# The first set of the second attention cut by units of 512 tokens, two of them spread by TensorE

## The chip, the cores and the metric

One core of a Trainium2 chip runs the whole program. The metric is device microseconds (us) for one execution; a kernel's figure is the median over its runs.

## The reference

Attention over a set of 32 learned points, and a gated feed-forward layer on its result:

```python
B, N, C, m = 4, 12416, 128, 32               # x (B, N, C), inducing I (m, C)
def mab(q, kv):                              # softmax attention, scale 1/sqrt(C)
    s = scale * (q @ kv.T); s = s - s.max(-1); a = exp(s); a /= a.sum(-1) + 1e-09
    return a @ kv
h = mab(I, x)                                # first attention:  32 points look at 12416 tokens
y = mab(x, h).reshape(B * N, C)              # second attention: each token looks at the 32 rows of h
xn = y / sqrt(mean(y * y, -1) + 1e-06) * rms_g
g, val = xn @ w_gate, xn @ w_val             # 128 -> 1536
out = (g * sigmoid(g) * val) @ w_out         # 1536 -> 128, float32, 49664 tokens
```

The weights arrive as 64-bit floats and are rounded to 32 bits in the kernel, by chunks of 512 columns.

## The kernel before

**Tiles.** A batch has 97 row tiles of 128 tokens, in 7 sets (five of 16 tiles, one of 15, one of 2). For the second attention and the feed-forward layer the sets are cut into units of 512 tokens or fewer: 25 in a batch, 100 in all. A unit's hidden columns come in 12 blocks of 128, so there are 1200 blocks.

**Second attention, folded.** `y` is never formed. With `a` the 32 attention weights of a token, the gate is `a @ (h * rms_g @ w_gate)`, so the kernel builds stacks `sg` and `sv` (`stack_of` L485, `stack_copy` L488, `stack_low` L492) that hold `h*g @ w_gate` and `h*g @ w_val`, an upper part and its remainder, and multiplies them with a unit's tile `a` of 128 partitions: upper, lower, upper and lower half of its 32 weights. The weights need no sum: the mean square of `y` goes through a 32x32 `gram` matrix (`square`, `times`, `total`, `clamp`), its power -0.5 is taken on GpSimd (`root`, L1032), and the weights are multiplied by it (`apply`, L1037).

**A block.** Gate matmul (L709), silu on ScalarE (L719), value matmul (L737), product on VectorE (L751), then the projection with `w_out`: either one plain f32 matmul (L807, kind P, two records) or, in the kinds S and D, three fp32r matmuls (L795, L796, L807) on parts that ScalarE (L764), VectorE (L770) and GpSimd (L815) prepare.

**Order.** Each engine takes its instructions in program order, and that order is written out by hand. The string `ORDER` in `first()` (from L890) lists every step up to the first block for batch 0: `t`/`a`/`v` transposes of x on TensorE and their copies on ScalarE/VectorE, `s` scores, `m` eviction with maximum, `e` exponentials, `r` transposes of them, `h` sums over tokens (`sum_h` L953), letters `p P u U g l j q` steps of the weights' rounding, then `fold`, `by` (`weigh` L966), `turn_h` (L972), `hT` (L977), and the second attention of set 0. That set is done here in two halves of 256 columns: `sc` (scores, L994), `T` (transpose, L998), `rm` (maximum, L1001), `sub` (L1006), `ex` (L1010), `ta`, `sq`, `zm`, `sm`, `mm` (L1029), `rt`, `ap`, `tb`, `hi`, `lo`. `sd` and `cp` spread unit 0 with a selection matrix on TensorE; `gather1` and `gather2` bring units 1 and 2 by DMA (`gather` L647: four transfers of 64 KB from the halves `hi` and `lo` on SyncE's queue, two each). Set 0's unit q consists there of the 32-partition groups q of all its columns.

What follows the first gate is given by long strings: `banks` (which bank of PSUM a step takes), `workers` and `outputs` (which buffer), `sorts` (the kind of each projection), `program` (one letter for each instruction of the blocks), and `taken` (which of the numbered small steps from `later()` and `seams()`, such as the weights' later chunks, other sets' second attention and the next batch's first attention, comes at each `.`). Each time a unit's tile is due, the iterator `gathered` gives the next unit to gather.

Of the kernel before, what the change touches and what calls it, by code (L numbers as in the profile page):

```python
# [23 lines left out]
def kernel(  # L24
# [101 lines left out]
    mhalf = small.tile([P, 16], F32, name="rt", bufs=1)  # L126
# [16 lines left out]
    sel = up.tile([P, 512], F32R, name="u", tag="u7")[:, 0:2 * P].rearrange("p (k r c) -> p k r c", k=2, r=R)  # L143
    nc.gpsimd.memset(sel.bitcast(F32), 0.0)
    for k in range(R):
        nc.gpsimd.tensor_copy(out=sel[:, k % 2, k, :], in_=ident[:, 0:m])
# [27 lines left out]
    def fetch_raw(i, c):  # L174
        if wide:
            raw[i, c] = words = places.pop(0).bitcast(I32)
            places.append(words.bitcast(F32))
            nc.sync.dma_start(out=words if i < 2 else words.rearrange("p (j c) -> p j c", j=512 // C),
                              in_=source(i, c).bitcast(I32))
# [8 lines left out]
    def rounding(i, c):  # L188
# [4 lines left out]
        def put():  # L193

            if i < 2:
                nc.sync.dma_start(out=w32[i][c][:], in_=st["dst"])
            if unread:
                fetch_raw(*unread.pop(0))
# [68 lines left out]
    NB, turn, turns, works, outs, factors = 5, [0], [], [int(c) for c in "01201212"], [int(c) for c in "01010"], []  # L267

    def bank():
        if turns:  # L270
            n = turns.pop(0)
        else:
            n = turn[0] % NB
            turn[0] += 1
        return pall[:, n, :]
# [8 lines left out]
    def attention(b, load_next):  # L284
# [129 lines left out]
        def scale_h():  # L414
            hg = st["hg"] = once.tile([P, P], F32, name="hg")
            nc.vector.tensor_scalar_mul(out=hg[:], in0=st["hT"][:], scalar1=gam)

        def square_h():

            if not b:  # L420
                scale_h()
# [217 lines left out]
    def gather(b, u):  # L639
# [4 lines left out]
        a = moving[b, u] = (xnp.tile([P, 512], F32R, name="xn1") if (b, u) == (0, 2) else  # L644
                            astk.tile([P, 512], F32R, name="a"))
# [210 lines left out]
    def store():  # L856
# [4 lines left out]
        if s == full:  # L861
            d = out[ds(b * N + start[s], P * per[s]), :].rearrange("(i w) c -> i w c", i=m)
        else:
            d = of(out, b, s)[q]
# [14 lines left out]
    GROUPS = ((0, 1, 2), (3, 4), (5, 6))  # L879
    ORDER = """  # L880
        open w3 t02 t00 t03 v00 t01 a01 a03 v02 t10 a10 t12 t13 s0 a12 a13 t11 t20 t21 a20 t23 m0 a23 t22 a22 a21 v11
        s1 t32 m1 t30 s2 a32 t33 t31 p00 P00 v30 u00 m2 own0 g00 Uv00 mB0 t40 l00 j00 q00 t42 nb0 a31 a33 t41 a40 v42 e0 t43
        s3 t51 a41 v43 s4 m3 e2 t52 t53 r0 t50 a51 m4 t60 own1 mB1 e1 a53 a50 a52 h0 r2 nb1 e3 p10 P10 r1 u10 U10 a60
        s5 h1 r3 m5 p20 e4 g10 s6 m6 h2 ls0 own2 mB2 u20 p11 nb2 ls1 r4 e5 least share r5 h3 h4 e6 ls2 shared fold h5
        r6 h6 l10 j10 q10 by0 by1 by2 P20 g20 u11 turn_h hT sc0z sc1z U20 l20 j20 q20 T0z rm0z sub0z ex0z T1z gram ta0z w7 sq0z rm1z
        sub1z ex1z zm0z ta1z sm0z st1 sq1z mm0z zm1z P11 silu sm1z mm1z rt0z rt1z p01 st0 U11 ap0z low0 tb0z
        ap1z hi0z tb1z lo0z w12 sd0z hi1z P01 cp0z lo1z w1 sd1z u01 cp1z w3 gather1 gather2
    """

    def first():  # L890

        V, S, G, T = nc.vector, nc.scalar, nc.gpsimd, nc.tensor
        st, at = f["st"], {}
# [5 lines left out]
        sums = pall[:, 7, :]  # L899
# [12 lines left out]
        def copy(copier, s, k):  # L912
            dst, src = at.pop(("turned", s, k))
            copier(out=dst, in_=src)
# [8 lines left out]
        def own_max(g):  # L923
            sets = GROUPS[g]
            t = at["own", g] = small.tile([P, R, R], F32, name="own")[:, :, 0:len(sets)]
# [3 lines left out]
        def spread_max(g):  # L929
            n = len(GROUPS[g])  # L930
            ps = bank()
            at["max"] = ps[:, 0:R * n]
# [3 lines left out]
        def bias_of(g):  # L936
            V.tensor_reduce(out=nb[:, g:g + 1], in_=at["max"], axis=AX.X, op=ALU.min)
# [9 lines left out]
        def sum_h(s):  # L947
# [3 lines left out]
            for t in range(per[s]):  # L951
                begin, end = (one[t % R] == (s, t) for one in ends)
                T.matmul(sums[ts(t % R, m), ts(group[s], C)], e[:, ts(t, m)], xn[:, t, :], start=begin, stop=end)  # L953
# [11 lines left out]
        def weigh(g):  # L965
            V.tensor_scalar(out=hs[:, ts(g, C)], in0=sums[:, ts(g, C)], scalar1=share[:, g:g + 1], scalar2=st["rl"][:],  # L966
                            op0=ALU.mult, op1=ALU.mult)

        def turn_h():
            ps = at["h"] = bank()  # L970
            for g in range(len(GROUPS)):
                T.matmul(ps[:, 0:P], hs[:, ts(g, C)], fold[:].rearrange("p q m -> p (q m)"), start=not g,  # L972
                         stop=g == len(GROUPS) - 1)

        def copy_h():
            hT = st["hT"] = once.tile([P, P], F32, name="hT")
            V.tensor_copy(out=hT[:], in_=at["h"][:, 0:P])  # L977

        H, HT = 2, per2[0] // 2
        a0 = {}  # L980

        def both(k):
            return slice(k * HT * m, (k + 1) * HT * m), slice(k * HT, (k + 1) * HT)

        def whole(name, make):
            if name not in a0:
                a0[name] = make()
            return a0[name]

        def scores2(k):  # L990
            cols, _ = both(k)
            ps = at["scores2", k] = bank()[:, 0:HT * m]
            for q in range(R):
                T.matmul(ps[ts(q, m), :], st["hT"][:, 0:m], xT[0, 0][:, q * per2[0] * m + cols.start:q * per2[0] * m + cols.stop],  # L994
                         start=True, stop=True)
# [4 lines left out]
        def row_max(k):  # L1000
            V.reduce_max(out=whole("mx", lambda: small.tile([P, 32], F32, name="mx2"))[:, both(k)[1]], in_=weights(0, 0)[:, both(k)[1], :],  # L1001
                         axis=AX.X)

        def sub_max(k):
            v = weights(0, 0)[:, both(k)[1], :]
            V.tensor_tensor(out=v, in0=v, in1=a0["mx"][:, both(k)[1]].unsqueeze(2).to_broadcast((P, HT, m)), op=ALU.subtract)  # L1006
# [5 lines left out]
        def turn_a(k):  # L1012
            V.transpose(out=whole("eT", lambda: worker([P, 512], F32, "eT"))[:, both(k)[0]], in_=sc[0][:, both(k)[0]])

        def square(k):
            ps = at["square", k] = bank()[:, 0:HT * m]
            T.matmul(ps, gram[0][:], a0["eT"][:, both(k)[0]], start=True, stop=True)

        def times(k):
            V.tensor_tensor(out=whole("z", lambda: worker([P, 512], F32, "z"))[:, both(k)[0]], in0=at.pop(("square", k)),  # L1020
                            in1=a0["eT"][:, both(k)[0]], op=ALU.mult)

        def total(k):
            V.reduce_sum(out=whole("ms", lambda: small.tile([P, 16], F32, name="ms"))[:, both(k)[1]],
                         in_=a0["z"][:, both(k)[0]].rearrange("p (t m) -> p t m", m=m), axis=AX.X, apply_transpose=True)

        def clamp(k):
            ms = a0["ms"][:, both(k)[1]]
# [466 lines left out]
```

## Time and profile before

| | |
|---|---|
| median of 3 runs | 1477.3 us (1476.86 to 1478.0) |
| the profiled execution's own time | 1478.17 us |
| its span in the trace | 1476.3 us |
| granted TensorE clock | 0.999 |
| TensorE matmul (PE) busy | 1464.3 us, 99%, 7290 instructions |
| VectorE (DVE) busy | 1428.1 us, 97%, 2484 |
| GpSimd (POOL) busy | 1366.7 us, 93%, 1197 |
| ScalarE (ACT) busy | 1302.0 us, 88%, 2596 |
| HBM | 53.95 MB read, 27.00 MB written |

PEld is TensorE's weight load, which runs beside its matmuls; SP is SyncE, and SPq, DVEq and so on are engines' DMA or instruction queues. "L709" is line 709 of the kernel. A row of the timeline has: start in us from the span's beginning, length, engine, line, operation, output<-input tile, shapes, a count where equal instructions follow each other, and in brackets how long the engine stood idle ahead of it and what ended that. A row with a count stretches from the first of the group to the last one's end, other instructions between them included. Busy time counts pipelined matmuls with modelled ends, so that 99% is not 99% of TensorE's peak.

### The profile page before, as it was taken

Reading aid. Unit: us, or ns where it says so; the run is one execution under the profiler, and the core shown is the slowest. Engines: PE = TensorE matmul, PEld = TensorE weight load, DVE = VectorE, ACT = ScalarE, POOL = GpSimd, SP = SyncE. Lnnn points to the kernel's source line nnn. Section 1 sums busy time; section 2 is a strip of 40 time slices with the busy share of each in tenths; the row PEclk is TensorE's granted clock in tenths of the full one; section 3 lists DMA queues with packets and bytes.
Section 4 is the critical chain, followed back from the end, with each engine's and each line's share of the span. In section 5 each row is a group of like instructions: output and inputs, shape, how many; then the busy total and the mean of one; then the engine's idle time right before and its main releaser. Section 6 shows DMA issues by size and latency. Waiting matters only on the chain.

```text
span 1476.3 us, 26012 instructions
## 1 busy us (share of the span) xinstructions
PE 1464.3 (99%) x7290; PEld 1102.3 (75%) x7290; DVE 1428.1 (97%) x2484; ACT 1302.0 (88%) x2596; POOL 1366.7 (93%) x1197
## 2 busy tenths in 40 slices
PE   9999999999999999999999999999999999999998
PEld 6566777877777777786777777777777777777787
DVE  6999999999999999999999999899999999999998
ACT  5798889889988889988988898988898999999997
POOL 1489998999999999999999999989989999999998
PEclk9999999999999999999999999999999999999999
DMA  7675324458544232455764212263332122122222
GB/s 286 130 118 104 64 43 94 88 124 130 84 85 79 36 65 37 99 132 106 125 106 99 44 37 36 44 135 91 74 63 46 33 37 43 37 39 41 42 39 34
DMA packets 391712, 116.28 MB, mean 79 GB/s; under 512 B 365584, under 2 KB 370704, under 8 KB 389008
## 3 DMA queue, kind: packets, MB, share of 16 engines
q1 hardware_dynamic: 390976, 114.55, 39.7%
q8 instruction: 58, 0.95, 0.3%
q14 instruction: 86, 0.70, 0.2%
q10 hardware_dynamic: 592, 0.08, 0.0%
HBM read 53.95 MB, written 27.00 MB: 55 GB/s over the span
## 4 chain that ended last, share of the span: by engine, by line
PE 95%; DVE 2%; ACT 1%; DMA 0%; issue 0%; POOL 0%; SPq 0%; DVEq 0%; POOLq 0%; ACTq 0%
PE gv L807 31%; PE gv L709 17%; PE gv L737 17%; PE gv L795 12%; PE gv L796 12%; PE gv L316 3%; PE gv L369 1%; PE gv L908 1%; DVE u L751 1%; PE gv L569 1%; PE gv L463 0%; PE gv L152 0%; DMA a<-lo 0%; POOL xn L815 0%; SPq L647 0%
## 5 line engine op out<-in xcount | busy, mean ns | idle before, releaser
L719 ACT ACTIVATE silu<-gv 128x512 f32<-128x512 f32 (+2 forms) x1200 | 673.8, 593 | 86.3 <-PE gv L709 69.6
L815 POOL TENSOR_TENSOR xn<-xn,xn 128x512 fp32r<-128x512 f32 (+2 forms) x467 | 579.1, 1256 | 22.4 <-PE gv L796 17.2
L709 PE MATMUL gv<-a,sg 128*128 128x512 f32 (+2 forms) x1188 | 482.1, 433 | 1.9 <-DMA a<-lo 1.5
L737 PE MATMUL gv<-a,sv 128*128 128x512 f32 (+2 forms) x1188 | 448.9, 410 | 0.2 <-ACT silu L719 0.2
L751 DVE TENSOR_TENSOR gv<-silu,gv 128x512 f32<-128x512 f32 (+2 forms) x658 | 431.4, 674 | 4.7 <-ACT silu L719 1.9
L764 ACT ACTIVATE xn<-gv 128x512 fp32r<-128x512 f32 (+2 forms) x633 | 371.0, 597 | 36.2 <-DVE gv L751 27.7
L751 DVE TENSOR_TENSOR u<-silu,gv 128x512 f32<-128x512 f32 (+2 forms) x542 | 345.4, 655 | 8.2 <-ACT silu L719 3.9
L807 PE MATMUL gv<-u,wo 128*128 128x512 f32 (+2 forms) x716 | 353.0, 577 | 0.1
L770 DVE SCALAR_TENSOR_TENSOR xn<-xn,gv 128x512 fp32r<-128x512 f32 (+2 forms) x520 | 339.6, 664 | 5.5 <-ACT xn L764 3.4
L709 PEld LDWEIGHTS gv<-a,sg 128*128 128x128 f32 x1188 | 223.6, 189 | 109.2 <-issue 36.6
L737 PEld LDWEIGHTS gv<-a,sv 128*128 128x128 f32 x1188 | 223.2, 189 | 85.8 <-issue 23.4
L815 POOL TENSOR_TENSOR xn<-xn 128x512 fp32r<-128x512 f32 (+2 forms) x216 | 268.8, 1252 | 9.1 <-PE gv L796 7.7
L777 POOL TENSOR_TENSOR xn<-u,xn 128x512 fp32r<-128x512 f32 (+2 forms) x163 | 202.1, 1245 | 13.6 <-ACT xn L761 9.2
L815 POOL TENSOR_TENSOR u<-xn,u 128x512 fp32r<-128x512 f32 (+2 forms) x130 | 163.2, 1260 | 2.6 <-PE gv L796 2.3
L795 PE MATMUL gv<-xn,xn 128*128 128x512 f32 (+2 forms) x430 | 163.5, 380 | 0.0
L807 PEld LDWEIGHTS gv<-u,wo 128*128 128x128 f32 x716 | 133.3, 190 | 28.3 <-issue 10.4
L807 PE MATMUL gv<-xn,xn 128*128 128x512 f32 (+2 forms) x366 | 141.1, 393 | 0.0
L796 PE MATMUL gv<-xn,xn 128*128 128x512 f32 (+2 forms) x366 | 136.5, 373 | 0.0
L795 PE MATMUL gv<-xn,more 128*128 128x512 f32 (+2 forms) x356 | 135.8, 381 | 0.0
L761 ACT ACTIVATE xn<-u 128x512 fp32r<-128x512 f32 (+2 forms) x180 | 111.9, 623 | 8.5 <-DVE u L751 7.7
L783 ACT ACTIVATE xn<-xn 128x512 fp32r<-128x512 f32 (+2 forms) x180 | 113.0, 632 | 3.3 <-POOL xn L777 2.7
L807 PE MATMUL gv<-xn,more 128*128 128x512 f32 (+2 forms) x304 | 115.5, 390 | 0.0
(223 smaller groups left out, 1833.7 us busy)
## 6 DMA issues: line engine op xcount, KB each, us to landing
out_dram<-o SPq DMA_DIRECT2D x320, 64.0 KB, 2.0
xT<-in_x_dram SPq DMA_DIRECT2D x60, 256.0 KB, 5.3
xn<-in_x_dram SPq DMA_DIRECT2D x60, 256.0 KB, 5.1
a<-hi SPq DMA_DIRECT2D x156, 64.0 KB, 2.0
a<-lo SPq DMA_DIRECT2D x156, 64.0 KB, 2.0
xn<-in_x_dram SPq DMA_DIRECT2D x5, 1024.0 KB, 9.5
xn<-w SPq DMA_DIRECT2D x18, 256.0 KB, 3.7
out_dram<-o SPq DMA_DIRECT2D x64, 60.0 KB, 2.0
```

The source lines that it names most:

```text
L709: nc.tensor.matmul(g[:, 0:T], stacks[b][0][:, ts(j, P)], halves_in_turn(one["a"][:, 0:T]), start=True, stop=True)
L719: nc.scalar.activation(sl[:, 0:T], gates.pop(n)[:, 0:T], AF.Silu)
L737: nc.tensor.matmul(v[:, 0:T], stacks[b][1][:, ts(j, P)], halves_in_turn(one["a"][:, 0:T]), start=True, stop=True)
L751: nc.vector.tensor_tensor(out=to, in0=sl[:, 0:T], in1=v[:, 0:T], op=ALU.mult)
L764: nc.scalar.activation(hi, t["u"], AF.Copy, scale=-(1.0 - 2.0 ** -13) * 2.0 ** -12)
L770: nc.vector.scalar_tensor_tensor(out=t["lo"], in0=t["hi"].bitcast(F32), scalar=4096.0, in1=t["u"], op0=ALU.mult, op1=ALU.add)
L777: nc.gpsimd.tensor_tensor(out=t["lo"], in0=t["u"], in1=t["hi"].bitcast(F32), op=ALU.subtract)
L783: nc.scalar.activation(t["hi"], t["hi"].bitcast(F32), AF.Copy, scale=-(2.0 ** -12))
L795: nc.tensor.matmul(to, weight_of(0, j), halves_in_turn(t["hi"]), start=not one["q"], stop=False)
L796: nc.tensor.matmul(to, weight_of(1, j), halves_in_turn(t["lo"]), start=False, stop=last)
L807: nc.tensor.matmul(to.rearrange("p (n h) -> p h n", h=2) if step2 else to, lhsT, rhs, start=one["left"] == NJ, stop=one["left"] == 1)
L815: nc.gpsimd.tensor_tensor(out=t["lo"], in0=t["hi"].bitcast(F32), in1=t["lo"].bitcast(F32), op=ALU.add)
```

## The change

All of it concerns the start up to the first blocks, and the lists.

- x's sets are loaded in the order 1, 2, 0, 3 to 6 with no weight chunk between them; five chunks follow (before: one behind set 3, four at the end). A chunk's second word load goes into the place of the first.
- `w11` instead of `w3`: eleven warm-up matmuls ahead of the first transposes. Transposes, copies and sums come in a new order, with a letter A, V or G for the engine of many steps.
- Three sums of the first attention: group 1's goes to another bank; the reciprocal of the softmax sum is multiplied into the fold matrix (`fold_r`), and the three shares are copied on ScalarE one by one (`share_h`), so that each needs only its own group; the copies `hT` and `hg` move to ScalarE.
- Set 0's second attention is cut by units: pieces 0 and 1 are units 0 and 1 (128 columns of 128 partitions each), piece 2 is units 2 and 3 (256 columns). A unit is now 512 tokens that follow each other, and so are its output rows. Pieces 0 and 1 are finished in `ORDER`; of piece 2 the scores, transpose, maximum, subtraction and exponential are there, and its further steps (`piece`) become ten small steps of the body, four of them on GpSimd.
- Units 0 and 1 are both spread by TensorE: four selection matrices per half (`sel[q, kind]`), eight matmuls of 128 columns for a unit, two copies. Units 2 and 3 are gathered by DMA, each by eight transfers of 32 partitions x 256 columns, where other units have four of 32 x 512.
- Subtractions of pieces 0 and 1 and the scaling of piece 1 are on GpSimd, and some lower halves on VectorE or GpSimd as the letters say. The table load for silu stands behind piece 0's upper half.
- `banks`, `workers`, `outputs`, `sorts`, `program` and `taken` are all new. Plain projections are 359 instead of 358, those of kind S 653 instead of 658, of kind D 188 instead of 184; the numbered steps are 879 instead of 871.

```diff
-    sel = up.tile([P, 512], F32R, name="u", tag="u7")[:, 0:2 * P].rearrange("p (k r c) -> p k r c", k=2, r=R)
+    sel = {}
+    for h, t in enumerate((up.tile([P, 512], F32R, name="u", tag="u7"), silp.tile([P, 512], F32R, name="silu"))):
+        nc.gpsimd.memset(t[:].bitcast(F32), 0.0)
+        picked = t[:].rearrange("p (q k r c) -> p q k r c", q=2, k=2, r=R)
...
@@ gather(b, u)
+        if (b, s) == (0, 0):
+            a = moving[b, u] = xnp.tile([P, 512], F32R, name="xn1") if u == 2 else astk.tile([P, 512], F32R, name="a")
+            for k, half in enumerate((hi, lo, hi, lo)):
+                for e in range(2):
+                    nc.sync.dma_start(out=a[ts(k, m), ts(e, w // 2)].bitcast(F32),
+                                      in_=half[ts(2 * (u - 2) + e, m), w // 2:w].bitcast(F32))
+            return
...
@@ output
-            d = of(out, b, s)[q]
+            d = out[ds(512 * u, 512), :].rearrange("(i w) c -> i w c", i=m)
@@ loads
-    for s in range(NS):
+    for s in (1, 2, 0, *range(3, NS)):
         load_rows(0, s)
-        for _ in range(1 if s == 3 else 4 if s == NS - 1 else 0):
+        for _ in range(5 if s == NS - 1 else 0):
             fetch_raw(*unread.pop(0))
@@ ORDER, from the last sum of the first attention on
-        r6 h6 l10 j10 q10 by0 by1 by2 P20 g20 u11 turn_h hT sc0z sc1z U20 l20 j20 q20 T0z rm0z sub0z ex0z T1z gram ta0z w7 sq0z rm1z
-        sub1z ex1z zm0z ta1z sm0z st1 sq1z mm0z zm1z P11 silu sm1z mm1z rt0z rt1z p01 st0 U11 ap0z low0 tb0z
-        ap1z hi0z tb1z lo0z w12 sd0z hi1z P01 cp0z lo1z w1 sd1z u01 cp1z w3 gather1 gather2
+        share shared tl r6 g10 spl rl U20A h4 q00 hs0A frA th0 u10 hs1A h6 l20 g20 U10A l10 hs2A th1 th2 hTA w2 sc0 p11
+        hgA sqh gc T0 rm0 sc1 j20 T1 sub0G ex0 rm1 sub1G sc2 T2 ta0 ex1 u11 ta1 st0 sq0 zm0 stc0 U11A q20 j10 q10 P11A
+        sm0 mm0V w1 sq1 rt0 rm2 zm1 sub2V sm1 ex2 mm1V w2 st1 stc1 ap0V tb0 hi0 low0 w4 sdh0 rt1 lo0V low1 sdl0 ap1G
+        sdm0 silu tb1 hi1 cpb0A p01 cpa0V lo1V P01A w1 sdh1 sdm1 sdl1 cpb1A cpa1A u01 U01V
@@ first()
-        def weigh(g):
-            V.tensor_scalar(out=hs[:, ts(g, C)], in0=sums[:, ts(g, C)], scalar1=share[:, g:g + 1], scalar2=st["rl"][:],
-                            op0=ALU.mult, op1=ALU.mult)
+        def fold_r(by):
+            copied(by, folded, fold[:].rearrange("p q m -> p (q m)"), st["rl"][:])
+        def share_h(by, g):
+            copied(by, hs[:, ts(g, C)], sums(g), share[:, g:g + 1])
...
-        H, HT = 2, per2[0] // 2
+        PARTS = (slice(0, 4), slice(4, 8), slice(8, 16))
...
+        def select(u, q, kind):
+            half = split_of[0, 0][kind][:, both(u)[0]]
+            T.matmul(at["spread", u, q // 2][:, ts(q % 2, P)], sel[q, kind], half, start=not kind, stop=bool(kind))
...
+        for engine_name, name, step, *args in (("DVE", "ta", turn_a), ("PE", "sq", square), ("DVE", "zm", times),
+                                               ("DVE", "sm", total), ("POOL", "mm", clamp, G), ("POOL", "rt", root),
+                                               ("POOL", "ap", apply, G), ("DVE", "tb", turn_b), ("ACT", "hi", upper),
+                                               ("POOL", "lo", lower, G)):
+            piece[name] = (engine_name, lambda step=step, args=args: step(*args, 2))
@@ later(0)
-            add(0, "DVE", f["stack_low"], 1, 0)
+            for name, (engine, step) in piece.items():
+                add(0, engine, step, call=(), key=("piece", 0, name))
@@ body
-    gathered = iter(flat[3:])
+    gathered = iter(flat[2:])
```

More of the change, by code (lines that the diff above doesn't have):

```diff
@@ L125 @@
     nc.vector.memset(ones, 1.0)
-    mhalf = small.tile([P, 16], F32, name="rt", bufs=1)
+    mhalf = const.tile([P, 16], F32, name="mhalf")
     nc.gpsimd.memset(mhalf[:], -0.5)
@@ L952, in sum_h @@
                 begin, end = (one[t % R] == (s, t) for one in ends)
-                T.matmul(sums[ts(t % R, m), ts(group[s], C)], e[:, ts(t, m)], xn[:, t, :], start=begin, stop=end)
+                T.matmul(sums(group[s])[ts(t % R, m), :], e[:, ts(t, m)], xn[:, t, :], start=begin, stop=end)
         def sum_l(g):
@@ L1012, in turn_a @@
         def turn_a(k):
-            V.transpose(out=whole("eT", lambda: worker([P, 512], F32, "eT"))[:, both(k)[0]], in_=sc[0][:, both(k)[0]])
+            e = whole(k, "eT", lambda: worker([P, 512], F32, "eT"))
+            V.transpose(out=e[:, both(k)[0]], in_=sc[0][:, both(k)[0]])
         def square(k):
-            ps = at["square", k] = bank()[:, 0:HT * m]
-            T.matmul(ps, gram[0][:], a0["eT"][:, both(k)[0]], start=True, stop=True)
+            ps = at["square", k] = bank()[:, 0:both(k)[0].stop - both(k)[0].start]
@@ L1051, in spread @@
[L1051 to L1059 removed]
+                split_of[0, 0] = [halves.tile([P, 512], F32R, name="hi")]
```

625 lines of the change are left out of this document (330 added, 295 removed), and 62 rows, old and new, of the table taken.

## The prediction

> **What bounds the kernel now.** I read the page first: busy shares, then the chain that ended last.
>
> ```profile
> span 1476.3 us, 26012 instructions
> PE 1464.3 (99%) x7290; PEld 1102.3 (75%) x7290; DVE 1428.1 (97%) x2484; ACT 1302.0 (88%) x2596; POOL 1366.7 (93%) x1197
> PE 95%; DVE 2%; ACT 1%; DMA 0%; issue 0%; POOL 0%; SPq 0%; DVEq 0%; POOLq 0%; ACTq 0%
> PE gv L807 31%; PE gv L709 17%; PE gv L737 17%; PE gv L795 12%; PE gv L796 12%; PE gv L316 3%; PE gv L369 1%; PE gv L908 1%; DVE u L751 1%; PE gv L569 1%; PE gv L463 0%; PE gv L152 0%; DMA a<-lo 0%; POOL xn L815 0%; SPq L647 0%
> ```
>
> 95% of the chain is TensorE. L709 and L737 are the 1200 gate and 1200 value matmuls: 17% of 1476.3 over 1200 is 0.21 us each, so in the body they follow each other without a wait that matters. A change can therefore win in three ways: the first gate matmul comes earlier, TensorE gets less to do, or it waits less. Next I read TensorE in order of time, from the warm-up matmuls to the first gates.
>
> ```profile
> 4.90 1.65 PE L152 MATMUL gv<-ident 128*128 128x128 f32 x6
> 6.34 1.98 PE L908 MATMUL gv<-ident,xn 128*128 128x128 f32 x16
> 8.80 1.50 PE L908 MATMUL gv<-ident,xn 128*128 128x128 f32 x12 [0.47 <-DVE xT L914]
> ...
> 31.34 1.29 PE L953 MATMUL gv<-xn,u 128*32 128x128 f32 x34
> 33.14 1.12 PE L972 MATMUL gv<-fold,u 128*128 128x128 f32 x6 [0.51 <-DVE u L966]
> 34.91 1.07 PE L994 MATMUL gv<-xT,hT 128*32 128x256 f32 x16 [0.65 <-DVE hT L977]
> ...
> 38.91 1.02 PE L485 MATMUL gv<-silu,hg 128*128 128x512 f32 x2
> 46.94 0.91 PE L709 MATMUL gv<-a,sg 128*128 128x512 f32 x3
> 47.78 1.06 PE L316 MATMUL gv<-xT,hT 128*32 128x512 f32 x8
> 49.81 0.45 PE L709 MATMUL gv<-a,sg 128*128 128x512 f32 x1 [0.55 <-DMA a<-lo]
> 50.10 1.08 PE L737 MATMUL gv<-a,sv 128*128 128x512 f32 x4
> 85.58 0.38 PE L709 MATMUL gv<-xn,sg 128*128 128x512 f32 x1
> ```
>
> Three stretches: the first attention, dense on TensorE, until about 32.6 (31.34 + 1.29); a serial chain to the first gate at 46.94; then a start that still stumbles, three gates and a wait for the DMA that brings unit 1. The row at 85.58 is the first gate of unit 2. The serial stretch is VectorE's, with one ScalarE and one GpSimd stop:
>
> ```profile
> 32.67 1.05 DVE L966 TENSOR_SCALAR u<-gv,nb,rl 128x128 f32<-128x128 f32 x3 [0.34 <-PE gv L953]
> 34.57 0.28 DVE L977 COPY hT<-gv 128x128 f32<-128x128 f32 x1
> 35.62 0.45 DVE L998 STREAM_TRANSPOSE sc<-gv 128x256 f32<-128x256 f32 x1 [0.16 <-PE gv L994]
> 36.10 0.42 DVE L1001 TENSOR_REDUCE mx<-sc 128x8 f32<-128x256 f32 x1
> 36.56 0.55 DVE L1006 TENSOR_TENSOR sc<-sc,mx 128x256 f32<-128x256 f32 x1
> ...
> 40.31 0.17 DVE L1029 TENSOR_SCALAR ms<-ms 128x8 f32<-128x8 f32 x1
> 42.26 0.43 DVE L1037 TENSOR_TENSOR sc<-sc,rs 128x256 f32<-128x256 f32 x1
> 43.18 0.69 DVE L492 TENSOR_TENSOR sg<-gv,sg 64x512 fp32r<-64x512 f32 x1 [0.49 <-ACT sg L488]
> ...
> 46.29 0.69 DVE L248 SCALAR_TENSOR_TENSOR we<-sg,we 128x512 int32<-128x512 int32 x1
> 50.78 0.69 DVE L751 TENSOR_TENSOR u<-silu,gv 128x512 f32<-128x512 f32 x1
> 37.20 0.42 ACT L1010 ACTIVATE sc<-sc 128x256 f32<-128x256 f32 x1 [5.68 <-DVE sc L1006]
> 37.53 0.77 ACT L430 ACTIVATE gram<-gv 32x32 f32<-32x32 f32 x4
> 41.18 1.28 ACT L1063 ACT_TABLE_LOAD   x1
> 40.56 3.28 POOL L1032 TENSOR_TENSOR rs<-ms,rt 128x8 f32<-128x8 f32 x2 [3.74 <-DVE ms L1029]
> ```
>
> **The change part by part.** I follow the new list of the start engine by engine, each step beginning when its inputs and its engine are there.
>
> Set order and whole loads: the transposes begin on set 1 after 11 instead of 3 extra warm-up matmuls. Each is two records, so 16 records are added. At the pace of the transposes (16 in 1.98 with the last one's end, 0.11 apiece start to start) they take 1.75, so the transposes begin at 8.1 instead of 6.34. But before, TensorE soon stood for set 1 (0.47 at 8.80) and idled for short waits later; the work from 6.34 to 32.6 is the same 97 transposes, 7 score sets and 97 sum tiles. From 26.3 us I take 1.2 for the quoted gap and for smaller waits (estimate 0.8 to 2.5), and find the last sum at 33.0 (32.2 to 33.7), 0.35 later than before. The Trainium skill (TensorE: Matmul & The Clock Gate, What's actually happening) says that the array runs at half rate until some 3.4 us of sustained work, with a phase that varies; the rows agree, with 0.21 us a record until 6.3 and 0.11 after.
>
> From the sum to the first transposed scores: before, three weighings on VectorE (1.05), three matmul pairs, a copy, scores of 256 columns; 32.65 to 35.62, 2.97 us. After, the reciprocal is folded into the fold matrix and two of three shares are done early; left are one ScalarE copy (0.3, behind a weight step of up to 0.5), one matmul pair (0.35), one copy (0.3) and half the scores (0.4), some 2.0 with hops. So the first transpose is at 35.0 instead of 35.62.
>
> From there to the gate, 11.3 us before (46.94 less 35.62). Now the first two pieces are 128 columns. VectorE's 256-column steps take 0.42 to 0.45 and its 128-column rows 0.28 to 0.35, so I take 0.28. Piece 0: transpose, maximum 0.6; subtraction on GpSimd 0.4 (0.3 to 0.65: three times VectorE's pace is the upper end); the exponential waits for the four L430 (0.77) and ends at 36.4; transpose behind piece 2's 0.45, 36.9; square behind one stack matmul (0.9; its two records are the row 38.91), 37.45; product, row sum, clamp 0.8, 38.3. The power is not seen at four columns; half of 1.64 is 0.8, all of it is the upper end; I take 0.9 since part of it will be fixed. While it runs VectorE does piece 2's maximum and subtraction and piece 1's sums (1.4), which are thus the later ones: scaling at 39.65, transpose, upper half 40.5. Then ScalarE loads its table and makes the one dummy silu, 1.5 us, to 41.95: it sits in the chain now, where before it lay under VectorE's and GpSimd's work. VectorE meanwhile does both stack remainders (0.69 each, L492) and the lower half. Piece 1's upper half 42.35, its lower half 43.0 behind one weight step, eight selecting matmuls and their loads 0.6: first gate at 43.7 (43.2 to 44.5). That is 3.2 us earlier (2.4 to 3.7).
>
> After the gate: before, from 46.94 to 50.10 TensorE did five gates (5 x 0.21) and one score set (1.0), 2.05 in 3.16 us, so it lost 1.1 to the DMA of unit 1. After, both units come from TensorE and both stacks are ready, so that wait goes (-1.1). What could be late next is VectorE's first product: its queue has six weight steps of 0.35 to 0.6 ahead (3.0 in sum), then the product at 46.4 instead of 50.78, and TensorE has eight matmuls and two score sets (3.7 us) until it needs it at 47.4. Covered.
>
> What TensorE has to do from the first gate on: the same 2400 gates and values. The kinds move by one (359 plain projections instead of 358, at other widths), worth 0.2, and piece 2's square comes over (0.25): +0.45. VectorE, which is full there, gets four steps of 256 columns (1.7) and gives back one 0.69 remainder and five low parts; GpSimd gets piece 2's clamp, power, scaling and lower half, some 3.
>
> Then units 2 and 3. Both now hang on piece 2, and each takes eight transfers of half the columns.
>
> ```profile
> 77.81 1.39 SPq L647 DMA_DIRECT2D a<-hi  x1
> 79.24 0.59 SPq L647 DMA_DIRECT2D a<-lo  x1
> ...
> 80.51 0.59 SPq L647 DMA_DIRECT2D a<-lo  x1
> 81.14 2.29 SPq L111 DMA_DIRECT2D xT<-in_x_dram  x2
> a<-lo SPq DMA_DIRECT2D x156, 64.0 KB, 2.0
> ```
>
> Eight times 0.59 is 4.7 us of SyncE, then 2.0 to land: 6.7. Before, unit 2 was gathered at 48 and its gate came at 85.58; these four rows were for unit 3, long ahead. After, VectorE's list has between its first product (46.4) and piece 2's last transpose 18 products (0.69 by the row, 0.60 start to start: 10.8), 15 weight steps (0.34 to 0.65: 7.4), four stack remainders (2.8) and nine others (4.3), 25.3 in sum; with some 2 of waits that is 74; upper and lower half on ScalarE and GpSimd 1.5; the gather runs from 76 to 83. Unit 2's first gate stands behind 24 gates, at 85.58 less 3.2 and less 1.1, plus some 2 us of projections that the new list puts ahead: about 83.5. Just in time. I charge 0.4 (0 to 6.7). The Trainium skill (DMA: Bandwidth & Descriptors, Rules for kernel authors) advises to coalesce, since transfers under 64 KB mostly pay overhead. The rows agree in that a 64 KB transfer costs its 0.59 and 2.0 at any moment; halved ones then double the issue, as I have charged.
>
> Sum: -3.2 - 1.1 + 0.45 + 0.4 = -3.45 us. The profiled execution took 1478.17, span 1476.3; the median is 1477.3, 0.9 under it. From the median: **1473.8 us**.
>
> **The rivals.**
>
> (1) *Half of it is lost; no measurable change.* TensorE is bound in the body, but VectorE is at 97% over the span. If the early gain meets VectorE's queue, which has work of 1.7 more early on, the 1.1 is not saved and 1.0 is paid again; with that -3.2 + 0.45 + 1.0 = -1.75, 1475.5. For it: 97%. Against: VectorE's own start moves by 4.4 (50.78 to 46.4), more than TensorE's. A mechanism for it is the port. By the row 42.26 a VectorE step with two SBUF inputs took 0.43 while the second power (42.2 to 43.84) ran on GpSimd, so I charge nothing for such pairs; if it had to wait for the power, the step would have ended at 44.2. The Trainium skill (SBUF — State Buffer, Who interferes with whom) has such pairs lock each other out for a whole instruction; the trace does not. By that rule piece 2's subtraction would wait behind the power and the gate would come some 0.9 later: 1474.7.
>
> (2) *The gather of unit 2 ends slower than before.* If the loads before it on SyncE (L111, 2.29 for two) and GpSimd's joins and power make the lower half late, TensorE stands at unit 2's first gate, with all else behind it in its queue. Fully exposed it costs 6.7, and unit 3's eight transfers behind it another 1.5 (4.7 less some three gates' worth of other work): -3.2 - 1.1 + 0.45 + 8.2 = +4.35, 1481.6. It turns slower than before from a lower half some 4 us later than my 76. For it: the margin is nothing. Against: piece 2's steps stand early in the lists.
>
> (3) *The start does not come earlier.* If the added warm-up matmuls run at the slow pace (0.21), the transposes begin at 9.8, 1.7 later, and the gate at 45.4: 1475.5. The change would then have done its chain but lost its front. The pace was already 0.11 from 6.34, so this is unlikely.
>
> **How the numbers follow.** The forecast, with the gain of the start kept: 0.60. The same with fewer small waits in the body (1471): 0.08. Rival 1: 0.12. Rival 2: 0.14. Rival 3: 0.06. Differences under 0.2% (2.95 us) are about what a measurement of this kernel can tell from no change, so the line lies at 1474.35, 0.55 above the forecast; I put 0.50 of its 0.60 under that line and 0.10 over it. Faster is 0.50 + 0.08 = 0.58, same 0.10 + 0.12 + 0.06 = 0.28, slower 0.14. Range: the low end has the gate at 43.2, no gather cost and some 2.5 us fewer small waits in a body of 1430 us whose lists are all new: 1470.0. The high end takes half of rival 2's 8.2 (-3.2 - 1.1 + 0.45 + 4.1 = +0.25) and the gate at 44.3 instead of 43.7 (+0.6): 1478.2.
>
> **What would show it.** Right: transposes from about 8.1, first transposed scores near 35.0, first gate at 43.2 to 44.5, no gap over 0.5 us on TensorE within the first eight gates, first product on VectorE near 46.4, unit 2's first gate at about 83.5 with no DMA named before it. Wrong: a gate after 45, a gap of over 2 us at unit 2 or 3, a power at four columns as long as at eight with VectorE waiting for it, or the gate early and the gain given back between 90 us and the end, which would make the equal body work the failed step.

## The result and the profile after

The changed kernel takes 1475.5 us (median of 21 runs, 1472.88 to 1477.49) against 1477.22 in the runs beside them (1476.43 to 1478.26): a ratio of 0.9985, 95% interval 0.9978 to 0.9992. It is faster, by half of what was forecast (1473.8), and inside the range. By the line that the prediction drew itself (1474.35) this counts as no measurable change, which it gave 0.28, and 1475.5 is the figure that it worked out for its rivals 1 and 3. Its times spread over 4.6 us, those of the kernel before over 1.8.

The page of the changed kernel: the span, the busy shares, and the chain that ended last.

```profile
span 1472.1 us, 26044 instructions
PE 1462.6 (99%) x7303; PEld 1105.9 (75%) x7303; DVE 1427.8 (97%) x2483; ACT 1305.7 (89%) x2604; POOL 1374.5 (93%) x1212
PE 96%; DVE 1%; DMA 1%; issue 0%; SPq 0%; POOL 0%; ACT 0%; DVEq 0%
```

TensorE still carries the chain. This execution took 1473.84, 4.2 less in span than before; it is one of the quicker ones. Its TensorE timeline, to be held against the stretches quoted in the prediction:

```profile
7.21 1.91 PE L934 MATMUL gv<-ident,xn 128*128 128x128 f32 x16
20.16 2.48 PE L934 MATMUL gv<-ident,xn 128*128 128x128 f32 x21 [0.30 <-DMA xn<-in_x_dram]
31.03 1.08 PE L978 MATMUL gv<-xn,u 128*32 128x128 f32 x32
38.58 0.49 PE L1049 MATMUL gv<-eT,gram 128*128 128x128 f32 x2 [0.80 <-DVE eT L1045]
45.05 1.00 PE L709 MATMUL gv<-a,sg 128*128 128x512 f32 x2
84.79 1.21 PE L709 MATMUL gv<-xn,sg 128*128 128x512 f32 x3
```

The front is as forecast (last sum ended at 32.87; 33.0 was said), with a wait for x's loads in it, 0.30 at 20.16. The first gate is at 45.05, not 43.7: outside the 43.2 to 44.5 that was said, and past the 45 that the prediction named as a sign of being wrong. Unit 2's first gate (the row at 84.79) names no DMA. VectorE and GpSimd between:

```profile
33.10 1.79 DVE L259 SCALAR_TENSOR_TENSOR o<-sc,o 128x512 f32<-128x512 uint32 x1
35.15 0.30 DVE L1028 STREAM_TRANSPOSE sc<-gv 128x128 f32<-128x128 f32 x1
36.93 1.37 DVE L244 TENSOR_SCALAR o<-sv 128x512 int32<-128x512 int32 x1
38.22 0.30 DVE L1045 STREAM_TRANSPOSE eT<-sc 128x128 f32<-128x128 f32 x1
39.68 0.41 DVE L1036 TENSOR_TENSOR sc<-sc,mx 128x256 f32<-128x256 f32 x1
47.73 1.28 DVE L751 TENSOR_TENSOR u<-silu,gv 128x512 f32<-128x512 f32 x2
33.07 1.27 POOL L265 TENSOR_TENSOR wo<-o,we 128x512 f32<-128x512 f32 x1 [3.80 <-DVE we L253]
36.75 1.27 POOL L265 TENSOR_TENSOR silu<-o,we 128x512 f32<-128x512 f32 x1
39.33 1.04 POOL L1066 TENSOR_TENSOR rs<-ms,mhalf 128x4 f32<-128x4 f32 x1 [1.31 <-DVE ms L1062]
```

Two VectorE steps are far too long. L259 took 1.79 us at 33.10 and 0.68 elsewhere, L244 took 1.37 at 36.93 and 0.42 elsewhere. Each lies beside a join of the weights on GpSimd (L265), and each ends a little less than its own normal length after that join does: at 34.89, 0.55 after 33.07 + 1.27, and at 38.30, 0.28 after 36.75 + 1.27. They look as if they had waited for it; two experiments below move the joins. A lower half (L1084, in the chain too) took 0.42 at 41.82 beside the scaling on GpSimd (41.69 to 42.09) and 0.28 at 43.98. The power at 39.33 held nobody: the subtraction with two SBUF inputs beside it took its 0.41.

The last view is TensorE by stretches of 4 us (stretch, its length, TensorE's busy time with its records, the granted clock, DMA share, GB/s), first in this execution, then in a second one of the same kernel that took 1472.9:

```profile
40.00:44.00 4.00, 3.17 (x21) 1.00 0.90 207
44.00:48.00 4.00, 3.80 (x16) 0.65 0.68 107
48.00:52.00 4.00, 4.00 (x23) 0.92 0.22 36
```

```profile
40.00:44.00 4.00, 3.17 (x21) 1.00 0.91 208
44.00:48.00 4.00, 3.81 (x26) 1.00 0.71 113
48.00:52.00 4.00, 4.00 (x21) 1.00 0.52 81
```

In the first, the clock lost (0.35 + 0.08) x 4 = 1.7 us, which is 3.4 us at half speed, just as the first gates began. The kernel before had its clock at 1.00 all through there.

### The profile page after: what moved, and what is told of

The parts are those of the page before. It is cut to its first block, busy times and chain, and to the rows that moved or that the text cites. A ratio compares the mean times of both kernels' runs of the same rounds, so it can differ in the third digit from the quotient of the medians.

```text
span 1472.1 us, 26044 instructions
## 1 busy us (share of the span) xinstructions
PE 1462.6 (99%) x7303; PEld 1105.9 (75%) x7303; DVE 1427.8 (97%) x2483; ACT 1305.7 (89%) x2604; POOL 1374.5 (93%) x1212
## 4 chain that ended last, share of the span: by engine, by line
PE 96%; DVE 1%; DMA 1%; issue 0%; SPq 0%; POOL 0%; ACT 0%; DVEq 0%
PE gv L807 32%; PE gv L709 17%; PE gv L737 17%; PE gv L795 12%; PE gv L796 12%; PE gv L316 3%; PE gv L369 1%; DMA xn<-in_x_dram 1%; PE gv L563 1%; PE gv L457 0%; PE gv L978 0%; SPq L104 0%; DVE o L259 0%; DVE u L751 0%; PE gv L934 0%
## 5 line engine op out<-in xcount | busy, mean ns | idle before, releaser
L815 POOL TENSOR_TENSOR xn<-xn,xn 128x512 fp32r<-128x512 f32 (+2 forms) x489 | 604.8, 1252 | 15.2 <-PE gv L796 10.3
L764 ACT ACTIVATE xn<-gv 128x512 fp32r<-128x512 f32 (+1 forms) x630 | 368.7, 597 | 31.9 <-DVE gv L751 26.0
L770 DVE SCALAR_TENSOR_TENSOR xn<-xn,gv 128x512 fp32r<-128x512 f32 (+2 forms) x508 | 332.0, 664 | 7.1 <-ACT xn L764 4.8
L815 POOL TENSOR_TENSOR xn<-xn 128x512 fp32r<-128x512 f32 (+2 forms) x185 | 232.5, 1260 | 7.5 <-PE gv L796 4.7
L815 POOL TENSOR_TENSOR u<-xn,u 128x512 fp32r<-128x512 f32 (+1 forms) x143 | 180.0, 1267 | 0.8 <-PE gv L796 0.7
L795 PE MATMUL gv<-xn,xn 128*128 128x512 f32 (+2 forms) x447 | 169.7, 380 | 0.0
L807 PE MATMUL gv<-xn,xn 128*128 128x512 f32 (+2 forms) x372 | 139.5, 386 | 0.0
L796 PE MATMUL gv<-xn,xn 128*128 128x512 f32 (+2 forms) x372 | 139.1, 374 | 0.0
L795 PE MATMUL gv<-xn,more 128*128 128x512 f32 (+2 forms) x341 | 131.3, 385 | 0.0
L761 ACT ACTIVATE xn<-u 128x512 fp32r<-128x512 f32 (+2 forms) x187 | 115.6, 619 | 9.6 <-DVE u L751 8.1
L783 ACT ACTIVATE xn<-xn 128x512 fp32r<-128x512 f32 (+2 forms) x187 | 116.3, 628 | 7.0 <-POOL xn L777 5.8
L807 PE MATMUL gv<-xn,more 128*128 128x512 f32 (+2 forms) x286 | 110.8, 392 | 0.0
```

The costliest lines, as they stand in the source:

```text
L764: nc.scalar.activation(hi, t["u"], AF.Copy, scale=-(1.0 - 2.0 ** -13) * 2.0 ** -12)
L770: nc.vector.scalar_tensor_tensor(out=t["lo"], in0=t["hi"].bitcast(F32), scalar=4096.0, in1=t["u"], op0=ALU.mult, op1=ALU.add)
L783: nc.scalar.activation(t["hi"], t["hi"].bitcast(F32), AF.Copy, scale=-(2.0 ** -12))
L795: nc.tensor.matmul(to, weight_of(0, j), halves_in_turn(t["hi"]), start=not one["q"], stop=False)
L796: nc.tensor.matmul(to, weight_of(1, j), halves_in_turn(t["lo"]), start=False, stop=last)
L807: nc.tensor.matmul(to.rearrange("p (n h) -> p h n", h=2) if step2 else to, lhsT, rhs, start=one["left"] == NJ, stop=one["left"] == 1)
```

## The experiments

Three questions: where the times of the changed kernel spread, what the two long VectorE steps cost, and how much room the gather has. Each ratio is to the kernel before, run beside it on the same chip; the runs were made on several chips.

**The same kernel again**, three times (no edit).

> The changed kernel once more, unchanged, to see where its executions differ (its times spread over 4.6 us, those of the kernel before over 1.8). Theory A, the front: x's loads, which ended last at 20.0 us in the first profile, land earlier or later; then the first gate moves with them by as much as the time does (45.05 us at a span of 1472.1; some 47 at a span of 1474.5), and the stretch from the first gate to the end stays 1427.0 us. Theory B, the body: the first gate stays within 0.3 us of 45.05, and the stretch after it changes by as much as the span.

> The same kernel a further time, with the same two readings: theory A, the first gate moves with the span and the stretch after it stays 1427.0 us; theory B, the first gate stays at 45.05 us and the stretch after it carries the difference.

again_a took 1474.3 with the first gate at 45.24 and the clock at half for 3.4 us from 45.6; again_b 1472.9 with the gate at 45.24 and no loss of clock (the two tables above are the first profile and again_b). So theory A falls for these two, and B names the place but not the cause: up to the gates both executions run alike, and a difference of 1.2 us is made within some fifteen gates and kept to the end (1.4 there).

> The changed kernel unchanged, timed on the same chip as the next two. Theory, the clock: its times spread over 2 us or more, from 1472.9 up, by whether TensorE loses half its clock at 43 to 51 us and by whether the clock comes late at the start (at 9 us instead of 4 to 6, as in one profile). Rival: they draw together within 0.7 us on this chip.

again_c: 1473.09 (11 runs, 1472.72 to 1476.2), six of them within 0.4 us at the lower end and the rest above, ratio 0.9978 (0.9970 to 0.9987). Its profiled execution (1475.39) shows a second source. The eleven warm-up matmuls ran at half pace:

```profile
5.24 4.52 PE L158 MATMUL gv<-ident 128*128 128x128 f32 x22
9.59 1.91 PE L934 MATMUL gv<-ident,xn 128*128 128x128 f32 x16
```

22 records in 4.5 us is 0.21 each. The transposes begin at 9.59, the gate comes at 46.56, 1.3 later than in again_b, and the loss of clock at the gates adds 1.2: at the end it is 2.5 behind. This is the prediction's rival 3 (9.8 for the transposes; the gate 1.7 later where 1.3 was measured), but as something that happens in some executions and not in others.

**Warm-up matmuls in the chain.**

```diff
-        sm0 mm0V w1 sq1 ... hi0 low0 w4 sdh0 rt1 lo0V low1 sdl0 ap1G
-        ... P01A w1 sdh1 sdm1 sdl1
+        sm0 mm0V w5 sq1 ... hi0 low0 w5 sdh0 rt1 lo0V low1 w2 sdl0 ap1G
+        ... P01A w2 sdh1 w1 sdm1 sdl1
```

> The changed kernel with nine more warm-up matmuls in the chain between 37 and 44.5 us (five instead of one ahead of piece 1's square, five instead of four ahead of the first selection, two ahead of unit 0's lower halves, two instead of one and one more among unit 1's). Theory, the clock: in three of four profiles of the changed kernel and its near variants TensorE was granted half its clock for 3.4 or 6.8 us from 43 to 45 us on, because it had stood idle in pieces since 37 us; busy, it keeps its clock, the granted clock is 1.0 from 40 to 60 us, gates stay at about 45.1, and the times draw together at 1472.9 (1472.5 to 1473.6), where the changed kernel alone spread from 1472.9 to 1477.5 about 1475.5. Rival, the spread has another cause: the median stays at 1475 to 1476, or rises by the added matmuls.

1473.14 (8 runs, 1472.9 to 1474.53; seven of the eight within 0.7), ratio 0.9974 (0.9964 to 0.9985). TensorE by stretches:

```profile
40.00:44.00 4.00, 4.00 (x28) 1.00 0.91 238
44.00:48.00 4.00, 3.98 (x27) 1.00 0.87 137
48.00:52.00 4.00, 3.97 (x24) 1.00 0.38 59
```

Kept busy, it kept its clock here, and the mean granted clock is 0.999 or 1.0 in all eight executions. The one slower time is the profiled execution, and there the front was late again (transposes at 9.70, the gate at 46.70), so more matmuls in the chain do not help against that.

**The same cover taken from the kernel before.**

```diff
-        ... ta0z w7 sq0z ... lo0z w12 sd0z ... cp1z w3 gather1 gather2
+        ... ta0z w1 sq0z ... lo0z w1 sd0z ... cp1z w1 gather1 gather2
```

> The kernel before with 20 of its 23 warm-up matmuls between 36 and 47 us taken out (one left at each of the three places). Theory, the clock: TensorE then idles over 1.5 us at 36.5 and over 2.5 us at 42, the granted clock falls to half for 3.4 or 6.8 us between 40 and 50 us in most executions, and the times spread upward from 1477.2 by 0.5 to 2.5 us, less than in the changed kernel where the first gates wait for the DMA of unit 1 anyway. Rival, they do nothing: 1477.2 within 0.4, clock 1.0.

1478.55 (10 runs, 1476.95 to 1479.53) against 1477.03; ratio 1.0008, interval 0.9999 to 1.0017, which just reaches no change. The edit takes out 19 of the 23 matmuls (not 20, as was said): 8 records are left of 46. The mean granted clock is 0.996 to 0.998 in all ten executions, against 0.999 to 1.0 in all 24 of the kernel before. The profile has the loss, in the stretch where the kernel before had none:

```profile
44.00:48.00 4.00, 1.56 (x8) 0.97 0.00 0
48.00:52.00 4.00, 3.88 (x14) 0.60 0.43 98
```

In this execution the clock also came late at the start (10.22 us), and the last sum ended at 33.97 instead of 32.62; so its later gate (48.27) isn't the price of the cover.

**Fewer warm-up matmuls at the front**, alone and with those in the chain.

```diff
-        open w11 t13 t11 t12 t10 c11A w1
+        open w3 t13 t11 t12 t10 c11A w1
```

> Three warm-up matmuls ahead of the first transposes, as before the change, in place of eleven. Theory, x's loads bound the front: the transposes begin at 5.5 instead of 7.2 us, TensorE waits longer for loads, the last transposes still begin at 20.0 to 20.3, the last sum ends within 0.3 us of 32.87 and the first gate is at 45.05 within 0.3. Rival, the prediction's term for the warm-ups: the last sum ends 0.5 to 1.2 us earlier, and the gate with it.

Alone: the last sum ended at 32.84 and the first transposed scores came at 35.12 (32.87 and 35.15 with eleven), which agrees with the theory that the loads bound the front, though the transposes began at 6.34, not at 5.5. A few tenths can't be told from one profile: the last sum ended at 32.87 to 33.48 in the profiles with eleven and a punctual front, at 32.40 to 33.29 in the four with three. The gate slipped to 45.64 as the clock fell at 44, for 6.8 us (0.51 and 0.64 in the two stretches from 44 on). 1473.93, 1472.77 to 1476.04 (10 runs).

> Nine more warm-up matmuls in the chain, as in the earlier run, and three instead of eleven ahead of the first transposes. Theory: the eleven cost 1.5 us only in those executions where the clock comes late (first transposes at 9.7), since otherwise x's loads bound the front; without them a late clock costs under 0.5, and the times lie within 0.8 us of each other, median 1472.7 to 1473.2. Rival, the eleven are needed for the clock further on: spread upward, median over 1473.5.

With those in the chain: 1472.37 (6 runs, 1472.13 to 1473.23), ratio 0.9969 (0.9957 to 0.9980), below the range expected; the times lie within 1.1 us, where 0.8 was said. This is the lowest median of all, 4.7 us under the kernel before; against the changed kernel, 1473.09 on that chip, the gain is not shown, since the intervals of the two overlap.

**The joins moved to VectorE.**

```diff
-                nc.gpsimd.tensor_tensor(out=st["dst"], in0=f[:], in1=e.bitcast(F32)[:], op=ALU.mult)
+                engine.tensor_tensor(out=st["dst"], in0=f[:], in1=e.bitcast(F32)[:], op=ALU.mult)
-        U10A l10 hs2A ... sc1 j20 T1 ... q20 j10 q10 P11A ... cpb0A p01 cpa0V lo1V P01A
+        U10A l10 J10V hs2A ... sc1 T1 ... q20 q10 P11A ... cpb0A cpa0V lo1V J20V p01
```

(With it two worker buffers, and two output buffers, change places in all lists.)

> The last two joins of the weights' rounding (L265) go from GpSimd to VectorE: one into VectorE's idle time at 33.8 us, one behind unit 1's lower half. Theory, a VectorE step between SBUF tiles stands still while GpSimd joins: the step L259 that took 1.79 us at 33.10 takes 0.68, the step L244 that took 1.37 at 36.93 takes 0.42, the first transposed scores come at 34.8 instead of 35.15, the first gate at 43.6 to 44.1 instead of 45.05, and the time is 1.0 to 1.4 us under that of the changed kernel. Rival, the two steps are long for another reason: they stay long, VectorE has 1.4 us more to do, the gate comes at 45.0 to 45.5 and the time does not fall.

The mechanism held; the two steps and the first transposed scores (34.95) came as expected:

```profile
33.27 0.69 DVE L259 SCALAR_TENSOR_TENSOR o<-sc,o 128x512 f32<-128x512 uint32 x1
36.73 0.39 DVE L244 TENSOR_SCALAR o<-sv 128x512 int32<-128x512 int32 x1
```

1473.76 (11 runs, 1473.62 to 1475.22), ratio 0.9978 (0.9969 to 0.9987). The gate came at 44.34, not at 43.6 to 44.1, with the clock lost for 6.8 us from 42.8. In these eleven a lower mean granted clock does not go with a longer time: the four at 0.998 took 1473.62, 1473.64, 1473.79 and 1475.22, the five at 1.0 took 1473.70 to 1474.27. The run with both edits shows the start better:

> Both at once: the two joins on VectorE and eight more warm-up matmuls in the chain. If both theories hold, the first gate comes at 43.9 to 44.4 with the clock at 1.0, and the time is 1472.9 less 1.0: 1471.5 to 1472.3, faster than both kernels. If the clock does not come from the idle time, 1473.5 to 1474.5, as with the joins alone.

The gate came at 44.16 with the clock at 1.0 as expected, and the time did not follow: 1473.76 (11 runs, 1473.3 to 1475.45). TensorE and VectorE say why:

```profile
44.16 0.65 PE L709 MATMUL gv<-a,sg 128*128 128x512 f32 x2
49.02 1.10 PE L807 MATMUL gv<-u,wo 128*128 128x512 f32 x2 [1.06 <-DVE u L751]
48.20 1.27 DVE L751 TENSOR_TENSOR u<-silu,gv 128x512 f32<-128x512 f32 x2
```

The first product is at 48.20, as in again_b (48.23): VectorE had the joins to do itself, and TensorE waits 1.06 us for it, all that the earlier gate had won. By the ninth gate this execution is even with again_b; a further 1.3 is lost from 335 us on (see the joins beside other work, below).

**The first product earlier in VectorE's list**: with the joins, the warm-ups and `w3`, the first `m` of the body's program moves ahead of two weight steps.

```diff
-        ..ggvs..v.gsgg.sg......m..msp.s....v
+        ..ggvs..v.gsmgg.sg........msp.s....v
```

> Joins on VectorE, warm-up matmuls in the chain, three at the front, and VectorE's first product moved ahead of two weight steps of the body's list (with the joins, TensorE waited 1.06 us at 47.95 for it). Theory, VectorE's queue took back what the earlier gate gave: the first plain projection comes at 47.6 to 48.1 instead of 49.0, and the time is 0.6 to 1.1 us under the run without the joins: 1471.9 to 1472.4. Rival, the gain is given back again within the next blocks, because VectorE has the joins' 1.4 us more to do: 1472.8 to 1473.6.

The first plain projection came at 47.70, but 1473.62 (9 runs, 1473.19 to 1474.29), the number of the rival. TensorE waited for VectorE at the next products, 0.26 and 0.28 us; of its lead of 1.27 over again_b at the fifth gate 0.1 was left at the ninth. The rest of the loss, 1.5, came in small steps later.

**The joins left on GpSimd, but beside other VectorE work.**

```diff
-        l10 hs2A ... sc0 p11 hgA ... sc1 j20 T1 sub0G ex0 rm1 sub1G sc2 ... ex1 u11 ta1 ... U11A q20 j10 q10 P11A
+        l10 j10 hs2A ... sc0 hgA ... sc1 T1 sub0G ex0 rm1 sub1G j20 sc2 ... ex1 ta1 ... q20 q10
-        tb0 hi0 low0 ... lo0V low1 ... silu tb1 hi1 cpb0A p01
+        tb0 hi0 p11 low0 ... lo0V u11 low1 ... silu P11A tb1 hi1 cpb0A U11A p01
```

(With it three warm-up matmuls at the front and more in the chain; two worker buffers change places.)

> With three warm-up matmuls at the front and more in the chain, as in the run that was fastest so far (1472.37), the two joins stay on GpSimd but are moved to where VectorE has only transposes, reductions and steps that read PSUM (one behind L259 at 33.8 us, one behind the subtractions at 36.7), and two weight steps of VectorE (L231, L244) move behind piece 0's last transpose. VectorE has no instruction more than in the changed kernel. Theory, the joins' hold on VectorE is a loss of VectorE's time as well as of the chain's: no VectorE step over 0.8 us between 33 and 44 us, the first gate at 43.4 to 44.2 with the clock at 1.0, the first product at 46.8 to 47.4 instead of 48.2, and the gain is kept: 0.7 to 1.2 us under 1472.4, 1471.2 to 1471.7. Rival, what the start gains meets another limit in the first blocks or later, as with the joins on VectorE: 1472.2 to 1473.8.

VectorE had no step over 0.8 us there and its first product came at 47.27, as expected. The joins now run beside transposes, reductions and PSUM reads, none of which is held up:

```profile
36.49 1.27 POOL L265 TENSOR_TENSOR wo<-o,we 128x512 f32<-128x512 f32 x1
36.91 0.31 DVE L1045 STREAM_TRANSPOSE eT<-sc 128x128 f32<-128x128 f32 x1 [0.31 <-ACT sc L1041]
37.19 0.29 DVE L1053 TENSOR_TENSOR eT<-gv,eT 128x128 f32<-128x128 f32 x1
37.51 0.31 DVE L1058 TRANSPOSE_TENSOR_REDUCE ms<-eT 128x4 f32<-128x128 f32 x1
44.33 0.65 PE L709 MATMUL gv<-a,sg 128*128 128x512 f32 x2
```

But the gate was at 44.33, above the 43.4 to 44.2 expected: VectorE's two moved steps (0.39 and 0.42) now stood in the chain. And the time was 1473.32 (7 runs, 1472.75 to 1473.73), ratio 0.9972 (0.9961 to 0.9983), nothing won against 1472.37. The profiled execution was 0.2 ahead of w3_warm's until 335 us and then lost 1.1 in steps of 0.1 to 0.35 at places (335, 653, 937, 1034 us) where the three kernels with joins on VectorE lose time as well, and where those with the lists' buffers unchanged lose none. These four have in common that two worker buffers change places. At the first of those places ScalarE starts a silu 0.28 us later, with nothing but its own last step named. What this is was not settled, and so the times of these four do not show what the joins' place alone is worth; the start of their profiles does.

**The gather, with twice the transfers.**

```diff
-                for e in range(2):
+                for e in range(4):
...
-                    nc.sync.dma_start(out=a[ts(k, m), ts(e, w // 2)].bitcast(F32), ...
+                    nc.sync.dma_start(out=a[ts(k, m), ts(e, w // 4)].bitcast(F32), ...
```

> The changed kernel with units 2 and 3 each gathered by sixteen transfers of 128 columns instead of eight of 256: SyncE's issue for a unit grows from 4.8 to 9.5 us. The prediction's rival 2 says that the gather has no room: unit 2's last transfer then lands at about 86.5 to 87 us, its first gate waits for the DMA by 2.5 to 3.5 us, unit 3's by up to as much again, and the time is 1476 to 1480 by the clock's state. If the room is larger than the trace says (82.0 landed, 83.8 to 84.8 used), TensorE names no DMA there and the time stays at 1473 to 1476.

1485.08, one execution. TensorE's waits from 50 to 130 us (us in total, times, longest):

```profile
PE gv L709 <- DMA xn<-lo: 2.9, 1, 2.9
PE gv L709 <- DMA a<-lo: 2.4, 1, 2.4
PE gv L737 <- DVE u L751: 1.8, 1, 1.8
```

Both waits came as priced, 2.9 at unit 2 and 2.4 at unit 3, but the whole cost 12 us against again_b, over twice their sum, beyond the 1476 to 1480 expected. Gate by gate it is 0.4 behind again_b at the 15th, 3.9 at the 25th, 7.1 at the 40th, 11.9 at the 75th and 12.2 at the end, so nearly all of it is lost by the 75th. TensorE's clock fell twice behind the waits, for 3.4 us each, at 87.8 and 125.3; the rest was not taken apart.

## Why the prediction was right, and where it was not

The way and the size are right within the range, but not by the prediction's sum. That sum is best held against again_b, an execution whose clock was kept. Spans: 1476.3 before, 1471.1 after, -5.2; the forecast was -3.45. Waits of TensorE are the time between two gates less its own work (0.215 us for a 512-column fp32r matmul, 0.86 for a plain projection, the rest by their kind); the 1171st gate is near the end. The differences between the columns rest on the records; the levels of waits and work also on these durations.

| term | predicted | again_b against before |
|---|---|---|
| first gate | -3.2 (43.7) | -1.7 (45.24 against 46.94) |
| waits, first to fifth gate | -1.1 | -1.1 (0.05 against 1.15) |
| waits, fifth to 1171st gate | +0.4 (the gather) | -2.5 (13.8 against 16.3) |
| TensorE's work | +0.45 | +0.1 (1376.2 against 1376.05) |

**The first gate** is the step that failed, and the term that failed in it is the port: "I charge nothing for such pairs". The walk without it was sound: from the last sum to the first transposed scores it said 2.0, and from there to the gate 8.7; with the joins off GpSimd and the clock kept (warm_joins and early) these were 1.9 and 8.8, in the changed kernel 2.3 and 9.9. The joins' hold is thus 0.4 and 1.1 us of the gate, 1.5 in all. (Its front is off by 0.2 in the sum alone: 8.1 + 26.3 - 1.2 is 33.2, not 33.0.) The prediction weighed the rule of the Trainium skill (SBUF — State Buffer, Who interferes with whom) against one row, the scaling at 42.26 beside a power, and let the row decide. The rule holds here for joins (two SBUF inputs on both engines, and VectorE's L244, an SBUF-to-SBUF TENSOR_SCALAR) and not for the power; whether that is for the power's operation or for its few elements (128x4, 128x8), no run separates. A row that showed it stood in the prediction itself: L1006 at 36.56 took 0.55 instead of 0.42, beside this one of the kernel before:

```profile
35.53 1.29 POOL L260 TENSOR_TENSOR wo<-o,we 128x512 f32<-128x512 f32 x1 [1.86 <-DVE o L254]
```

The kernel's text has it as well: its body orders GpSimd's next step behind such steps of the weights, for the reason "no two at the shared port"; the start, where the change put the joins into the chain, has no such order.

**The early wait** went as said, and what could have come next, VectorE's first product (46.4 said, 47.7 to 48.2 measured), stayed covered; it ceased to be covered when the gate came another 1.1 earlier, in the runs with the joins on VectorE. So rival 1's mechanism is real, one microsecond further on than where the change ended.

**The gather** was just in time: "76 to 83" was 75.1 to 82.0 in again_b, and unit 2's first gate, 83.5 said, came at 83.77. Rival 2 was rightly left a rival, but it was probably priced too low: doubling the issue cost 12 us in the one execution made, where full exposure was put at 8.2.

**The waits of the body** fell by 2.5 us where nothing was forecast (a chance of 0.08 was given to it). 1.4 of it is gone by the 25th gate, with VectorE's own start 2.6 us earlier; some 2.7 goes between the 400th gate and the 602nd, of which the kernel before spent 1.1 on a late gather at its 601st (779.71 us), and some 1.6 comes back elsewhere. That the new lists do it is argued, not shown.

**The clock** was in no term. The prediction used the Trainium skill (TensorE: Matmul & The Clock Gate, What's actually happening) for the first 6 us alone. The same section of the Trainium skill says that the activity window is free-running, 3413 ns long. The records of the granted clock agree: granted at 4.25, fallen at 45.20, 12 x 3.413 later, for one window or two. Before, 46 records of warm-up matmuls covered the serial chain from 36 to 47 us; the change has 16 there, and TensorE idles in pieces from 36.9 to 44.5 (the longest 0.80 by the row at 38.58). That the cover matters is shown both ways, by more of it in the changed kernel and less in the kernel before; what decides between one execution and the next is not, and again_b kept its clock with the same pieces. The loss costs 1.0 us in the first profile, and with a clock that comes late at the start 2.5 in again_c. The median of the 21 runs lies 2.6 us above an execution where neither happens (1475.5 against 1472.9). That these two make up the 2.6 is likely but argued: the four quickest of the 21 have a mean granted clock of 1.0 and the five slowest 0.997 or 0.998, but one of 1476.0 has 1.0 as well, and of the 21 only the one of 1473.84 has a trace. In again_c, on another chip, the same kernel's median was 1473.09.

So that the number came out near was luck, by a sum in which three things missed: the joins' hold (+1.5), fewer waits (-2.5, and the 0.4 charged for the gather), and what lies between again_b and the median (+2.6, the clock as far as is known). The profile of before took 0.9 more than its median, so -5.2 in span is -4.3 in the times, and with these 2.6 it is the -1.7 measured.

## What to carry to other kernels

Idle time of TensorE in a serial stretch ahead of dense matmuls can cost the first of them their clock, as it did here; shorten the chain and keep the cover, and look at the granted clock in windows of a few microseconds, in more than one execution, when times spread upward from a sharp lower edge. Price a GpSimd step beside VectorE by what each reads, not by the first overlapping pair that looks harmless, and try it where VectorE transposes, reduces or reads PSUM: that freed VectorE here, though the time did not fall. A gain at the start counts only as far as the next engine in line, here VectorE, can follow.

## What the runs showed of the hardware that was not expected

The changed kernel's clock fell though TensorE had no idle gap over 0.81 us in the chain; the runs do not show the share of a window that decides. GpSimd's power of 128x4 took 1.04 us where 128x8 took 1.64; on a straight line through the two, 0.44 is independent of the size (an estimate; the prediction took 0.9), and it held up no VectorE step. A wait of 2.9 us at one unit and 2.4 at the next went with a loss of 12, in one execution.
